# Partial logits and two ranking products moved to GpSimd, the gate's broadcast to ScalarE, fewer instructions for the gate's denominator

## The chip, the cores and the metric

The kernel runs on one core of a Trainium2 chip. A core has five engines that run their own instruction streams in program order and meet through semaphores: TensorE (PE; its weight loads are listed as PEld), VectorE (DVE), ScalarE (ACT), GpSimd (POOL) and SyncE (SP), whose queue issues most transfers. The metric is the device time of one execution in microseconds (us).

## The reference

Two stages with the arrays in fp32. The first is an attention through 32 memory slots for 8 batches and 8 heads of 576 positions; the second is a mixture of 8 experts in which every one of the 4608 tokens goes to the one expert with the largest logit.

```python
# attention, per batch and head
a = softmax(phi)                       # over the 576 positions
k_m, v_m = a.T @ k, a.T @ v            # 32 x 64 each
x = softmax(q @ k_m.T / 8) @ v_m       # over the 32 slots
# experts, on x as 4608 x 512
logits = x @ w_gate
e_idx = argmax(logits, axis=1)
probs = exp(logits - logits.max()); probs /= probs.sum() + 1e-9
gate_w = probs[e_idx]
eom = 1 / (1 + exp(-(x @ w_output_gate)))
out[t] = gate_w[t] * eom[t, e] * (relu(x[t] @ w1[e]) @ w2[e])
```

The factor of a token's row is therefore 1 / ((sum of exp(logit - max) + 1e-9) * (1 + exp(-z))), with z the chosen expert's output-gate logit.

## The kernel before

**Attention.** Batches are handled in four pairs (index `bp`), each in five steps of 256 or 128 positions, so 20 steps (`t` counts them, three more drain the pipeline). For one step `scores` makes the scores on PE; `shift` (lines 866 to 872) turns them by a VectorE transpose, takes a maximum on VectorE (L870) and subtracts it on GpSimd (L872); `expo` (L876) takes the exponential on ScalarE; `divide` (L882 to L885) sums and inverts on VectorE and multiplies on GpSimd (L885); `back` (L890) transposes back; `values` (L903, L905) multiplies by the value memories on PE and copies the result, `xo`, to SBUF on ScalarE; `store` (L1014, L1018) writes it to the scratch `xs` in DRAM. A row of `xs` has four quarters of 144 columns: 128 of x and 16 partial logits (8 of the gate, 8 of the output gate). `memory` meanwhile makes the next pair's memories (`kvm`, L782, on ScalarE; `ve_b`, L784, on GpSimd; two memsets, L727 and L728).

**Logits.** The 16 logits of a token are the sum of its four partial ones. `store` defers that sum (L1022, VectorE) by eight items of the list `ORDER`; it is then emitted right behind the next step's `shift`, and, for the last step of a pair, at once at the end of the step.

**Ranking.** After the last step of a pair, `rank(bp)` works out each token's expert (`oh`, one-hot), its place among that expert's tokens (`pr` on PE, L956 to L960), and its factor `gd`, which is copied to 16 columns (`gt`, L981) and written by four DMAs over the columns 128 to 143 of the first quarter in `xs` (L983, L986), where the experts' stage reads only column 128. It also makes nine 128 x 128 matrices `Aw` on GpSimd (L988). It is a generator: every `yield` gives the turn back to the rest of the program. For the second pair it is driven eight turns at the head of the next attention step, ahead of that step's `shift`; for the third it is driven by `hook`, two turns behind three items of attention. With the second and third pair runs `route_early`, which from `Aw` and the counts makes the lists of tokens (`table`, L233 to L250) by which the first blocks' rows are gathered (L538, GpSimd).

**Experts.** A block is up to 384 tokens of one expert; its rows are gathered from `xs`, transposed on PE (L1089), split into a high and a low part, and multiplied by weights that are split in the same way (`whl`: ScalarE L577, VectorE L591). L1241 is the first layer's matmul, L1278 the second's. The first block starts inside the attention's last part, so that the rest of the attention and of the ranking is emitted between the experts' matmuls. Since every engine works in program order, an instruction that waits holds all that stand behind it on its engine.

```python
ORDER = ["R4", "W", "X", "S", "R0", "m", "D", "M", "B", "V0", "R1", "R1", "V1", "M", "m", "C"]
LATE = {"lg": 8, "w": 2, "ct": 8, "pe": 3, "dve": 2}
```

In `ORDER`, R is turns of the ranking, X `expo`, S `shift`, D `divide`, B `back`, V `values` and `store`, C the next `scores`, m and M the memories.

Of the kernel before, what the change touches and what calls it, by code (L numbers as in the profile page):

```python
# [8 lines left out]
F32 = mybir.dt.float32  # L9
# [3 lines left out]
AF = mybir.ActivationFunctionType  # L13
ALU = mybir.AluOpType
AX = mybir.AxisListType
PSUM = bass.MemoryType.PSUM

P = 128
B, H, S, D, M = 8, 8, 576, 64, 32
NTOK, DM, E, F = 4608, 512, 8, 1024  # L20
NBP = B // 2
NCH = 9
# [37 lines left out]
XQ = 144  # L60
# [7 lines left out]
def attention_moe(tc, phiT, kv, qT, wgo, wall, out):  # L68
    nc = tc.nc
    V, A, G, T = nc.vector, nc.scalar, nc.gpsimd, nc.tensor  # L70

    with contextlib.ExitStack() as ctx:
        cp = ctx.enter_context(tc.tile_pool(name="cp", bufs=1))
        dp = ctx.enter_context(tc.tile_pool(name="dp", bufs=1, space=bass.MemoryType.DRAM))
        xs = dp.tile([NTOK, XROW], F32, name="xs")
# [27 lines left out]
        rt = ctx.enter_context(tc.tile_pool(name="rt", bufs=1))  # L103
# [52 lines left out]
        wg = cp.tile([P, H, 16], F32, name="wg")  # L156
        nc.sync.dma_start(wg[64:128], wgo)

        ohg = rt.tile([P, NCHT, E], BF16, name="ohg", bufs=1)
        jg = rt.tile([P, NCHT], I32, name="jg", bufs=1)  # L160
        Aw = rt.tile([P, NCHT, P], BF16, name="Aw", bufs=1)
# [299 lines left out]
        def take_pr():  # L461

            while taken:
                yield
            taken.append(1)

        def hold(n):

            if "open" not in env:
                return  # L470
            end = clock[0] + n
            while clock[0] < end:
                yield
# [433 lines left out]
        def rank(bp, lg):  # L907

            t0 = bp * 2 * S
            lt = lg[:, :, 0:E]  # L910
            lo = lg[:, :, E:2 * E]
            b3 = [P, NCH, E]
            cs = slice(bp * NCH, (bp + 1) * NCH)
            lm = rt.tile([P, NCH], F32, name="lm")
            w1_ = rt.tile(b3, F32, name="w1_")
            w2_ = rt.tile(b3, F32, name="w2_")
            w3_ = rt.tile(b3, F32, name="w3_")
            pm = rt.tile([P, NCH], F32, name="pm")
            zs = rt.tile([P, NCH], F32, name="zs")
            gd = rt.tile([P, NCH], F32, name="gd")  # L920
            oc = rt.tile([P, E], F32, name="oc")
            rki = rt.tile([P, NCH], I32, name="rki")
            ri = rt.tile([P, NCH], I32, name="ri")
            row = rt.tile([P, NCH], F32, name="row")
            gt = rt.tile([P, NCH, XQ - P], F32, name="gt")
            oh = ohg[:, cs]
            dscb = desc[:].unsqueeze(1).to_broadcast(b3)
            lmb = lm[:].unsqueeze(2).to_broadcast(b3)
            V.tensor_reduce(lm[:], lt, axis=AX.X, op=ALU.max)
            yield  # L930
            V.tensor_tensor(w1_[:], lt, lmb, ALU.is_ge)
            G.tensor_tensor(w2_[:], lt, lmb, ALU.subtract)
            yield
            V.tensor_tensor(w1_[:], w1_[:], dscb, ALU.mult)
            yield
            V.tensor_reduce(pm[:], w1_[:], axis=AX.X, op=ALU.max)
            yield
            V.tensor_tensor(oh, dscb, pm[:].unsqueeze(2).to_broadcast(b3), ALU.is_equal)
            yield
            V.tensor_reduce(oc[:], oh.rearrange("p c e -> p e c"), axis=AX.X, op=ALU.add)  # L940
            V.tensor_tensor(w3_[:], oh, lo, ALU.mult)
            A.activation(w2_[:], w2_[:], AF.Exp)
            yield
            if bp:
                V.tensor_tensor(ohcs[bp][:], ohcs[bp - 1][:], oc[:], ALU.add)
            else:
                V.tensor_copy(ohcs[bp][:], oc[:])
            V.tensor_reduce(zs[:], w3_[:], axis=AX.X, op=ALU.add)
            yield

            def rest():
                yield from take_pr()
                yield from hold(LATE["pe"])

                pr = ps_r.tile([P, NCH, E], F32, name="pr")
                T.matmul(pr[:], strict[:], oh, start=True, stop=False)  # L956
                if bp:
                    T.matmul(pr[:], ones_b[:], ohcs[bp - 1][:].unsqueeze(1).to_broadcast(b3), start=False, stop=False)
                for c in range(1, NCH):
                    T.matmul(pr[:, c:], ones_b[:], oh[:, 0:NCH - c], start=False, stop=(c == NCH - 1))  # L960
                yield
                V.tensor_reduce(gd[:], w2_[:], axis=AX.X, op=ALU.add)
                A.activation(zs[:], zs[:], AF.Exp, scale=-1.0)
                yield
                yield from hold(LATE["dve"])
                V.tensor_tensor(w1_[:], oh, pr[:], ALU.mult)
                taken.clear()
                V.tensor_scalar(gd[:], gd[:], 1e-9, None, ALU.add)
                yield
                with nc.allow_low_precision("whole numbers"):  # L970
                    V.tensor_reduce(rki[:], w1_[:], axis=AX.X, op=ALU.add)
                V.tensor_scalar(zs[:], zs[:], 1.0, None, ALU.add)
                yield
                V.tensor_scalar(ri[:], rki[:], 127, None, ALU.bitwise_and)
                V.tensor_scalar(jg[:, cs], rki[:], 7, None, ALU.arith_shift_right)
                V.tensor_tensor(gd[:], gd[:], zs[:], ALU.mult)
                yield
                V.tensor_copy(row[:], ri[:])  # L978
                V.reciprocal(gd[:], gd[:])
                yield  # L980
                V.tensor_copy(gt[:], gd[:].unsqueeze(2).to_broadcast([P, NCH, XQ - P]))  # L981
                for b in range(2):
                    nc.sync.dma_start(  # L983
                        xs[t0 + b * S:t0 + b * S + 512, P:XQ].rearrange("(c p) d -> p c d", p=P),
                        gt[:, 4 * b:4 * b + 4])
                    nc.sync.dma_start(xs[t0 + b * S + 512:t0 + b * S + 576, P:XQ], gt[64 * b:64 * b + 64, 8])  # L986
                for c in range(NCH):
                    (G if AWP else V).tensor_scalar(  # L988
                        Aw[:, bp * NCH + c], iota_row[:], row[:, c:c + 1], None, ALU.is_equal)
                    if c % 3 == 2:  # L990
                        yield
                ranked.append(bp)

            yield from together(route_early(bp - 1) if bp in (1, 2) else route_late() if bp == NBP - 1 else (), rest())

        ranked = []

        def together(*gens):

            gens = [iter(g) for g in gens]  # L1000
            while gens:
                for g in list(gens):
                    try:
                        next(g)
                    except StopIteration:
                        gens.remove(g)
                yield

        def store(bp, c2, xo, lg):
            t0 = bp * 2 * S  # L1010
            b, n = c2 // 2, 2 if c2 < 4 else 1
            if c2 < 4:
                r = t0 + b * S + (c2 % 2) * 256
                nc.sync.dma_start(xs[r:r + 256].rearrange("(c p) d -> p c d", p=P),  # L1014
                                  xo[:].rearrange("p c r d -> p c (r d)"))
            else:
                for b_ in range(2):
                    nc.sync.dma_start(  # L1018
                        xs[t0 + b_ * S + 512:t0 + b_ * S + 576],
                        xo[64 * b_:64 * b_ + 64, 0].rearrange("p r d -> p (r d)"))  # L1020
            xl = xo[:].rearrange("p c r (g d) -> p c (r g) d", g=2)[:, 0:n, :, P:XQ]
            defer("lg", lambda: V.tensor_reduce(  # L1022
                lg[:, 2 * c2:2 * c2 + n], xl.rearrange("p c q l -> p c l q"), axis=AX.X, op=ALU.add))

        def last(g):
            r = None
# [70 lines left out]
        def defer(nm, f):  # L1097
            deferred.append([LATE[nm], f])
# [15 lines left out]
        def attention():  # L1114
# [8 lines left out]
            for t in range(NT + LAG["V"]):  # L1123
# [45 lines left out]
                if g >= 0 and g % 5 == 4:  # L1169
                    bp = g // 5  # L1170
                    undefer(99)
                    left.append(bp)
                    rou.finish()
                    if bp < NBP - 1:
                        rou = Side(rank(bp, lgs[bp]))
                    else:
                        late.gens.append(rank(bp, lgs[bp]))
# [216 lines left out]
        n = NPE + NPT + NPP  # L1394
# [52 lines left out]
```

## Time and profile before

| | |
|---|---|
| median of 3 runs | 553.92 us (553.5 to 554.93) |
| the profiled execution's own time | 553.22 us |
| its span, first to last instruction | 551.5 us |
| PE busy | 507.9 us, 92% of the span |
| DVE busy | 354.1 us, 64% |
| ACT busy | 288.0 us, 52% |
| POOL busy | 231.8 us, 42% |
| mean granted TensorE clock | 0.97 |

A share of busy time is a mean over stages, so the stages are read one by one: a line of digits has the span in 40 slices of 13.8 us, each digit the busy share in tenths. A row of the timeline has the start, the length, the engine, the line of the program, the operation, the tile written and those read, and in square brackets how long the engine stood idle before it and who released it.

### The profile page before, as it was taken

Reading aid. Unit: us, or ns where it says so; the run is one execution under the profiler, and the core shown is the slowest. Engines: PE = TensorE matmul, PEld = TensorE weight load, DVE = VectorE, ACT = ScalarE, POOL = GpSimd, SP = SyncE. Lnnn points to the kernel's source line nnn. Section 1 sums busy time; section 2 is a strip of 40 time slices with the busy share of each in tenths; the row PEclk is TensorE's granted clock in tenths of the full one; section 3 lists DMA queues with packets and bytes.
Section 4 is the critical chain, followed back from the end, with each engine's and each line's share of the span. In section 5 each row is a group of like instructions: output and inputs, shape, how many; then the busy total and the mean of one; then the engine's idle time right before and its main releaser. Section 6 shows DMA issues by size and latency. Waiting matters only on the chain. (4 is left out here: it accounts for less than half of the span.)

```text
span 551.5 us, 10575 instructions
## 1 busy us (share of the span) xinstructions
PE 507.9 (92%) x3859; PEld 439.1 (80%) x3859; DVE 354.1 (64%) x779; ACT 288.0 (52%) x536; POOL 231.8 (42%) x254
## 2 busy tenths in 40 slices
PE   3788767689999999999999999999999999999993
PEld 2555545469789889898898989898999899888982
DVE  4376687877866659997454564954786387629310
ACT  3467465545535455553444545854785386548310
POOL 2244374860444134510467472655447363821101
PEclk9969799979999999999999999999999999999997
DMA  8999999995567756973466574876686577743001
GB/s 306 419 391 386 408 356 372 302 413 170 152 185 219 248 162 226 315 201 117 149 183 204 173 239 129 247 217 217 176 259 188 189 236 245 220 151 98 30 21 43
DMA packets 41998, 123.54 MB, mean 224 GB/s; under 512 B 10256, under 2 KB 10320, under 8 KB 41552
## 3 DMA queue, kind: packets, MB, share of 16 engines
q1 hardware_dynamic: 35136, 102.71, 56.5%
q0 software_dynamic: 6800, 20.06, 10.2%
q8 instruction: 32, 0.52, 0.4%
q14 instruction: 30, 0.25, 0.2%
HBM read 102.40 MB, written 20.35 MB: 223 GB/s over the span
## 5 line engine op out<-in xcount | busy, mean ns | idle before, releaser
L1278 PE MATMUL bps<-whl,hh 128*128 128x512 f32 x640 | 192.4, 393 | 0.0
L1241 PE MATMUL bps<-xh,whl 128*128 128x384 f32 x640 | 165.8, 336 | 0.0
L591 DVE TENSOR_TENSOR whl<-w,whl 128x1024 fp32r<-128x1024 f32 x112 | 138.2, 1239 | 10.9 <-ACT whl L577 10.8
L1278 PEld LDWEIGHTS bps<-whl,hh 128*128 128x128 f32 x640 | 119.9, 188 | 24.3 <-issue 0.2
L577 ACT CAST whl<-w 128x1024 fp32r<-128x1024 f32 x112 | 116.5, 1045 | 21.2 <-PE bps L1278 16.5
L1241 PEld LDWEIGHTS bps<-xh,whl 128*128 128x128 f32 x640 | 115.8, 188 | 1.1 <-ACT hh L1245 0.4
L532 POOL DMA_INDIRECT xg<-xs,idx_ql x84 | 97.3, 1158 | 25.6 <-issue 23.5
L1241 PE MATMUL bps<-xl,whl 128*128 128x384 f32 x320 | 107.0, 334 | 0.0
L1278 PE MATMUL bps<-whl,hl 128*128 128x512 f32 x240 | 93.7, 390 | 0.0
L1246 DVE SCALAR_TENSOR_TENSOR hl<-bps,hh 128x384 fp32r<-128x384 f32 x80 | 44.0, 554 | 60.3 <-ACT hh L1245 60.3
L1245 ACT ACTIVATE hh<-bps 128x384 fp32r<-128x384 f32 x80 | 38.9, 492 | 76.2 <-PE bps L1241 76.1
L1214 POOL DMA_INDIRECT out<-y,idx_ol x23 | 25.2, 1095 | 110.6 <-ACT y L1213 54.3
L1241 PEld LDWEIGHTS bps<-xl,whl 128*128 128x128 f32 x320 | 60.1, 188 | 0.3
L1278 PEld LDWEIGHTS bps<-whl,hl 128*128 128x128 f32 x240 | 45.1, 188 | 8.5
L1236 PE MATMUL bps<-xh,whl 128*128 128x384 f32 x128 | 37.7, 338 | 0.0
L872 POOL TENSOR_TENSOR ea<-ea,mx 128x512 f32<-128x512 f32 (+1 forms) x20 | 19.2, 960 | 43.3 <-DVE mx L870 39.0
L1237 PE MATMUL bps<-xh,whl 128*128 128x256 f32 x128 | 35.7, 279 | 0.0
L1213 ACT ACTIVATE y<-bps,gx 128x512 f32<-128x512 f32 x19 | 13.1, 687 | 40.0 <-PE bps L1278 33.4
L905 ACT COPY xo<-bpd 128x576 f32<-128x576 f32 x36 | 22.2, 641 | 21.4 <-PE bpd L903 9.7
L903 PE MATMUL bpd<-ve_b,aT 64*128 64x144 f32 (+1 forms) x320 | 28.6, 331 | 3.4 <-DVE ea L866 3.2
L1214 POOL DMA_INDIRECT out<-y,idx_ob x9 | 10.1, 1119 | 49.8 <-ACT y L1213 37.8
L988 POOL TENSOR_SCALAR Aw<-iota_row,row 128x128 bf16<-128x128 bf16 x36 | 26.0, 738 | 8.9 <-DVE row L978 8.9
(267 smaller groups left out, 588.2 us busy)
## 6 DMA issues: line engine op xcount, KB each, us to landing
w<-wall SPq DMA_DIRECT2D x112, 512.0 KB, 4.4
kvt<-kv SPq DMA_DIRECT2D x32, 512.0 KB, 8.1
xs<-xo SPq DMA_DIRECT2D x16, 576.0 KB, 7.4
qt<-qT SPq DMA_DIRECT2D x16, 512.0 KB, 8.5
ph<-phiT SPq DMA_DIRECT2D x3, 1152.0 KB, 11.7
kv<-kv SPq DMA_DIRECT2D x4, 512.0 KB, 8.5
xg<-xs,idx_ql POOLq DMA_INDIRECT x84, 4.5
ph<-phiT SPq DMA_DIRECT2D x4, 288.0 KB, 3.2
```

The costliest lines, as they stand in the source:

```text
L532: G.indirect_dma_start(out=z["xg"][:, k, XQ * b:XQ * b + XQ], out_offset=None, in_=xs[0:z["rows"]].rearrange("t (a q) -> (t a) q", a=4), i ...
L577: A.copy(hl[:, 0], w[:])
L591: V.tensor_tensor(hl[:, 1], w[:], hl[:, 0].bitcast(F32), ALU.subtract)
L903: T.matmul(px[to:to + n, r, sl], z["aT"][h, o:o + n], ves[2 * bp + b][h, g], start=True, stop=True)
L988: (G if AWP else V).tensor_scalar(Aw[:, bp * NCH + c], iota_row[:], row[:, c:c + 1], None, ALU.is_equal)
L1214: G.indirect_dma_start(out=out, out_offset=bass.IndirectOffsetOnAxis(ap=z["idx"][1][0:n, z["q0"] + k:z["q0"] + k + 1], axis=0), in_=y[0:n] ...
L1236: T.matmul(pb, w[:, 0, o:o + P], x[0][:, cc], start=(cc == 0), stop=False)
L1237: T.matmul(pb[:, 0:256], w[:, 1, o:o + P], x[0][:, cc, 0:256], start=False, stop=(cc == 3))
L1241: T.matmul(pb, w[:, b, o:o + P], x[a][:, cc, 0:n_], start=(n == 0), stop=(n == 11))
L1245: A.activation(h_[:, j], pb, AF.Relu)
L1246: V.scalar_tensor_tensor(l_[:, j], pb, 0.0, h_[:, j].bitcast(F32), ALU.max, ALU.subtract)
L1278: T.matmul(py[k], a, w[:, b, DM * f:DM * f + DM], start=(u == 4 and f == 0 and n == 0), stop=(u == 7 and f == 1 and n == len(ps) - 1))
```

## The change

The sum of the partial logits becomes two additions on GpSimd. In `rank`, the product of the maximum's mask with `desc` and the product of `oh` with the output-gate logits go from VectorE to GpSimd. The exponentials `w2_` get a ninth column per token chunk, which holds 1e-9 from the start, so that the sum over nine has the denominator; `1 +` and the product for the factor become one instruction. The broadcast `gt` has 4 columns instead of 16 and is made on ScalarE; the four DMAs write 4 columns.

```diff
+        w2t = rt.tile([P, NCH, E + 1], F32, name="w2t", bufs=1)
+        V.memset(w2t[:, :, E:], 1e-9)
...
-            G.tensor_tensor(w2_[:], lt, lmb, ALU.subtract)
-            yield
-            V.tensor_tensor(w1_[:], w1_[:], dscb, ALU.mult)
+            G.tensor_tensor(w2_, lt, lmb, ALU.subtract)
+            yield
+            G.tensor_tensor(w1_[:], w1_[:], dscb, ALU.mult)
...
-            V.tensor_tensor(w3_[:], oh, lo, ALU.mult)
+            G.tensor_tensor(w3_[:], oh, lo, ALU.mult)
...
-                V.tensor_reduce(gd[:], w2_[:], axis=AX.X, op=ALU.add)
+                V.tensor_reduce(gd[:], w2s[:], axis=AX.X, op=ALU.add)
...
-                V.tensor_scalar(gd[:], gd[:], 1e-9, None, ALU.add)
...
-                V.tensor_scalar(zs[:], zs[:], 1.0, None, ALU.add)
...
-                V.tensor_tensor(gd[:], gd[:], zs[:], ALU.mult)
+                V.scalar_tensor_tensor(gd[:], zs[:], 1.0, gd[:], ALU.add, ALU.mult)
...
-                V.tensor_copy(gt[:], gd[:].unsqueeze(2).to_broadcast([P, NCH, XQ - P]))
+                A.copy(gt[:], gd[:].unsqueeze(2).to_broadcast([P, NCH, 4]))
...
-            defer("lg", lambda: V.tensor_reduce(
-                lg[:, 2 * c2:2 * c2 + n], xl.rearrange("p c q l -> p c l q"), axis=AX.X, op=ALU.add))
+            def logits():
+                half = rt.tile([P, 2, 2, XQ - P], F32, name="half", bufs=1)[:, 0:n]
+                G.tensor_tensor(half, xl[:, :, 0:2], xl[:, :, 2:4], ALU.add)
+                G.tensor_tensor(lg[:, 2 * c2:2 * c2 + n], half[:, :, 0], half[:, :, 1], ALU.add)
+
+            defer("lg", logits)
```

No `yield` is added or taken away.

## Rows read from the trace of the kernel before

**Rows 1.** The span in 40 slices, from the page: PE's busy tenths.

```profile
PE   3788767689999999999999999999999999999993
```

**Rows 2.** Busy time of the engines in four stretches. Columns: stretch and length, then for PE, PEld, DVE, ACT and POOL the busy us and (x) the number of instructions, then the granted clock, the DMA engines' mean busy share and the GB/s.

```profile
61.50:85.00 23.50, 18.47 (x324) 12.93 (x324) 18.01 (x52) 14.30 (x36) 14.14 (x20) 0.79 1.02 370
85.00:119.00 34.00, 24.71 (x444) 17.03 (x436) 31.37 (x93) 18.44 (x38) 22.38 (x28) 0.90 0.98 358
119.00:160.00 41.00, 40.16 (x299) 34.11 (x298) 32.63 (x84) 20.24 (x34) 16.41 (x20) 1.00 0.61 189
160.00:545.00 385.00, 382.59 (x2082) 347.25 (x2080) 239.28 (x461) 201.41 (x352) 157.02 (x140) 1.00 0.59 185
```

**Rows 3.** Timeline of VectorE around the start of the second pair's ranking.

```profile
86.67 0.36 DVE L1022 TENSOR_REDUCE lg<-xo 128x32 f32<-128x128 f32 x1
...
87.84 0.65 DVE L890 STREAM_TRANSPOSE aT<-ea 128x512 f32<-128x512 f32 x1
88.46 0.26 DVE L1022 TENSOR_REDUCE lg<-xo 128x16 f32<-128x64 f32 x1
88.75 0.23 DVE L929 TENSOR_REDUCE lm<-lg 128x9 f32<-128x72 f32 x1
89.02 0.80 DVE L931 TENSOR_TENSOR w__1397<-lg,lm 128x72 f32<-128x72 f32 x1
...
90.12 0.23 DVE L936 TENSOR_REDUCE pm<-w__1397 128x9 f32<-128x72 f32 x1
...
91.25 0.71 DVE L866 STREAM_TRANSPOSE ea<-bpd 128x512 f32<-128x512 f32 x1
...
94.07 0.23 DVE L190 TENSOR_TENSOR tge<-pr,thr_e 128x104 f32<-128x104 f32 x1
```

**Rows 4.** Timeline of GpSimd over the same stretch and on to the first gathers.

```profile
86.89 1.05 POOL L872 TENSOR_TENSOR ea<-ea,mx 128x512 f32<-128x512 f32 x1 [3.46 <-DVE mx L870]
88.00 0.31 POOL L727 MEMSET a<- 64x256 f32 x1
...
88.63 1.04 POOL L885 TENSOR_TENSOR ea<-ea,sa 128x512 f32<-128x512 f32 x1
89.64 0.34 POOL L932 TENSOR_TENSOR w__1398<-lg,lm 128x72 f32<-128x72 f32 x1
...
97.71 5.50 POOL L988 TENSOR_SCALAR Aw<-iota_row,row 128x128 bf16<-128x128 bf16 x9
...
103.75 1.04 POOL L885 TENSOR_TENSOR ea<-ea,sa 128x512 f32<-128x512 f32 x1
105.31 1.25 POOL L538 DMA_INDIRECT xg<-xs,idx_ga  x1 [0.52 <-DVE i L248]
...
109.20 1.05 POOL L872 TENSOR_TENSOR ea<-ea,mx 128x512 f32<-128x512 f32 x1
```

**Rows 5.** Timeline of PE: three places of the same stretch at which it waited.

```profile
91.20 0.17 PE L276 MATMUL pr<-ohc,ones_b 128*128 128x8 bf16 x1 [1.69 <-DVE ohc L945]
...
94.35 0.19 PE L956 MATMUL pr<-ohg,strict 128*128 128x72 bf16 x1 [0.78 <-DVE tge L190]
...
111.22 0.59 PE L791 MATMUL bpa<-ident,kvm 128*128 128x128 f32 x2 [2.58 <-ACT kvm L782]
```

**Rows 6.** Timeline of ScalarE in the second pair's ranking.

```profile
94.14 0.21 ACT L963 ACTIVATE zs<-zs 128x9 f32<-128x9 f32 x1
95.50 0.64 ACT L905 COPY xo<-bpd 128x576 f32<-128x576 f32 x1 [1.14 <-PE bpd L903]
96.27 0.62 ACT L782 ACTIVATE kvm<-pk,rs 128x128 f32<-128x128 f32 x2
```

**Rows 7.** Busy time in stretches, columns as in rows 2: a short idle time of PE, a longer one, and what followed the longer one.

```profile
89.50:91.20 1.70, 0.01 (x2) 0.03 (x1) 1.56 (x8) 0.78 (x2) 0.48 (x2) 1.00 1.03 415
...
108.70:111.20 2.50, 0.00 (x0) 0.00 (x0) 2.50 (x1) 1.61 (x4) 2.47 (x3) 1.00 1.00 386
111.20:118.90 7.70, 6.61 (x61) 4.42 (x62) 7.15 (x15) 4.36 (x10) 4.29 (x5) 0.56 1.03 416
```

**Rows 8.** Timelines of VectorE, GpSimd and PE in the third pair's ranking, which lies inside the experts' stage.

```profile
137.41 0.22 DVE L934 TENSOR_TENSOR w__2048<-w__2048,desc 128x72 f32<-128x72 f32 x1
137.67 0.23 DVE L936 TENSOR_REDUCE pm<-w__2048 128x9 f32<-128x72 f32 x1
...
139.75 0.79 DVE L938 TENSOR_TENSOR ohg<-desc,pm 128x72 bf16<-128x72 f32 x1
...
137.64 1.05 POOL L872 TENSOR_TENSOR ea<-ea,mx 128x512 f32<-128x512 f32 x1 [4.30 <-DVE w__2048 L934]
...
140.60 0.19 PE L956 MATMUL pr<-ohg,strict 128*128 128x72 bf16 x1 [0.25 <-DVE ohg L938]
```

**Rows 9.** Timelines of VectorE in the first pair's ranking, and of GpSimd behind the first pair's `Aw`.

```profile
61.53 0.26 DVE L1022 TENSOR_REDUCE lg<-xo 128x16 f32<-128x64 f32 x1 [4.25 <-ACT xo L905]
...
69.22 0.23 DVE L966 TENSOR_TENSOR w__950<-ohg,pr 128x72 f32<-128x72 bf16 x1 [0.67 <-PE pr L960]
...
79.25 1.04 POOL L872 TENSOR_TENSOR ea<-ea,mx 128x512 f32<-128x512 f32 x1
```

**Rows 10.** The group of the logit sums, from the groups by line: count, then busy us and mean ns of one, then the idle time before them and its releaser.

```profile
L1022 DVE TENSOR_REDUCE lg<-xo 128x32 f32<-128x128 f32 (+1 forms) x20 | 6.8, 341 | 4.3 <-ACT xo L905 4.3
```

**Rows 11.** Busy time in one stretch, columns as in rows 2: the two microseconds in which the first pair's factors are being written.

```profile
80.00:82.00 2.00, 0.74 (x4) 0.40 (x4) 1.07 (x4) 1.14 (x3) 2.00 (x4) 0.85 1.03 245
```

More of the change, by code (lines that the diff above doesn't have):

```diff
@@ L915, in rank @@
             w1_ = rt.tile(b3, F32, name="w1_")
-            w2_ = rt.tile(b3, F32, name="w2_")
+            w2s = w2t
+            w2_ = w2s[:, :, 0:E]
             w3_ = rt.tile(b3, F32, name="w3_")
@@ L924, in rank @@
             row = rt.tile([P, NCH], F32, name="row")
-            gt = rt.tile([P, NCH, XQ - P], F32, name="gt")
+            gt = rt.tile([P, NCH, 4], F32, name="gt")
             oh = ohg[:, cs]
@@ L940, in rank @@
             V.tensor_reduce(oc[:], oh.rearrange("p c e -> p e c"), axis=AX.X, op=ALU.add)
-            V.tensor_tensor(w3_[:], oh, lo, ALU.mult)
-            A.activation(w2_[:], w2_[:], AF.Exp)
+            G.tensor_tensor(w3_[:], oh, lo, ALU.mult)
+            A.activation(w2_, w2_, AF.Exp)
             yield
@@ L980, in rest @@
                 yield
-                V.tensor_copy(gt[:], gd[:].unsqueeze(2).to_broadcast([P, NCH, XQ - P]))
+                A.copy(gt[:], gd[:].unsqueeze(2).to_broadcast([P, NCH, 4]))
                 for b in range(2):
                     nc.sync.dma_start(
-                        xs[t0 + b * S:t0 + b * S + 512, P:XQ].rearrange("(c p) d -> p c d", p=P),
+                        xs[t0 + b * S:t0 + b * S + 512, P:P + 4].rearrange("(c p) d -> p c d", p=P),
                         gt[:, 4 * b:4 * b + 4])
-                    nc.sync.dma_start(xs[t0 + b * S + 512:t0 + b * S + 576, P:XQ], gt[64 * b:64 * b + 64, 8])
+                    nc.sync.dma_start(xs[t0 + b * S + 512:t0 + b * S + 576, P:P + 4], gt[64 * b:64 * b + 64, 8])
                 for c in range(NCH):
```

## The prediction

> **What bounds the kernel now.** I read the page's 40 slices first [rows 1]: PE's digit is 6 to 8 in the early slices and 9 nearly throughout the rest. Then the windows [rows 2]: from 160 to 545 us PE is busy 382.59 of 385 us, so there whatever VectorE or GpSimd saves or loses is worth nothing unless PE stands still for it. PE idles before 119 us: 9.3 us between 85 and 119 (34.00 less 24.71), where VectorE is busy 31.37 of 34. So the time is the moment at which the experts' matmuls start (119 us) plus nearly fixed PE work, plus any hole that the change puts into PE later. The DMA engines are full up to 119 us (share 0.98 and 1.02), but the waits of PE in the stretch are on VectorE and ScalarE [rows 5], so I read the three timelines instruction by instruction.
>
> The chain from 85 us on is this. VectorE runs without a gap from L1022 to L190 [rows 3]. PE waits for it twice, at 91.20 for the counts (1.69 us) and at 94.35 for L190, which frees the bank `pr` [rows 5]. Behind L956 on PE stands `values`, then ScalarE's `xo` (95.50) and `kvm` (96.27) [rows 6], then GpSimd's L784 and the nine `Aw` (97.71), then the lists and the gathers (105.31), then L872 (109.20) [rows 4], whose exponential holds the `kvm` for which PE waits 2.58 us at 111.22 [rows 5]. What delays L190 delays the first expert matmul one for one.
>
> **Prices.** On GpSimd a product of 72 columns takes 0.34 us, a 256-column memset 0.31 [rows 4]. The new additions have 64 and 32 columns; I take 0.30 each, 0.6 a pair (bounds 0.5, a little under the memset for both, and 0.7, two products). On VectorE the sum that goes cost 6.8 us in 20 [rows 10], some 0.27 us of pitch each. The product by `desc` costs VectorE 0.22 [rows 8] against 0.34 on GpSimd. The Trainium skill (GPSIMD Engine Reference, 4.1 Engine selection) puts two-input elementwise work about two times slower on GpSimd than on VectorE; these rows have one and a half times. By the rule the product would be 0.45 and the sum below 0.2 us higher.
>
> **Part by part.** (a) *Before 85 us: -0.3 us.* In the first pair's ranking the maximum waits for two additions instead of one sum (+0.4) and then for the product's detour (+0.2). But VectorE waited 0.67 us for PE at 69.22 [rows 9], and that hides both. Behind it three small instructions and a sum leave VectorE ahead of `Aw`, whose end releases L872 at 79.25 [rows 9], so that chain comes some 0.3 us earlier (bounds 0 and -0.6). The additions behind that L872 lengthen GpSimd's own row of work, but nothing waits for its end before 85 us.
>
> (b) *Second pair's ranking: +1.8 us.* On GpSimd the order will be: L872, ending 87.94; the pair of additions for 86.67's sum, 88.54; the two memsets (0.63 from 88.00 to 88.63), 89.17; L885, 1.01, 90.18; the pair for 88.46's sum, 90.78; and only then can L929 start on VectorE, at 90.85 instead of 88.75 [rows 3, 4]: +2.1. VectorE is through with L890 by 88.2 and stands idle, with the whole ranking and the next `shift` (91.25) queued behind. L931 then no longer runs beside L885, so its 0.80 falls to some 0.23, but the product by `desc` must wait for L932 on GpSimd (0.34 + 0.34): from L929 to L936 it takes 1.07 us instead of 1.37, -0.3. The other product costs nothing net: 0.14 us leave VectorE and a wait of that size for GpSimd comes in. Left is +1.8 at L866, and the same at L190. Bounds: 1.4 (0.5 a pair, no latency) and 2.2.
>
> (c) *Behind it: +0.3 us.* The copy to `gt` is put into ScalarE's stream between `xo` and `kvm` (nearest row, L963 with 9 columns, 0.21 [rows 6]): +0.2, bounds 0 and 0.3. A pair of additions lies ahead of L885 at 103.75 and so of the gathers; they waited 0.52 for the lists there [rows 4], so of 0.6 some 0.1 shows (bounds 0 and 0.2).
>
> (d) *The clock: +0.6 us.* PE's idle time before L276 grows from 1.69 to some 3.4 us. After the 1.70 us without PE work from 89.50 the clock stayed at 1.00, while behind the 2.50 us from 108.70 it was 0.56 on average for 7.7 us, that is mostly the lower level of 1.2 GHz [rows 7]. So I expect the matmuls between L276 and L956 to run partly at 1.2 GHz. From 91.20 on PE had 3.41 us of work in 4.2; twice that time would be hidden in part by L190, which is late by 1.8 itself. Bounds 0 and 1.9; I take 0.6, a third, because L190 hides the first part.
>
> (e) *Third pair's ranking: +1.4 us.* It is in the experts' stage, where PE has no slack: already now L956 waited for `oh` at 140.60 [rows 8]. `hook` emits `shift` and then the ranking, so on GpSimd the product by `desc` stands behind L872 (137.64 to 138.69) and ends at 139.03; L936 starts at 139.1 instead of 137.67, with L1246, L882 and L938 behind it on VectorE. `oh` is 1.4 us later, and PE has nothing else to do ahead of L956. Bounds 1.1 and 1.7. What waits on the weights' split behind it moves with PE and costs nothing more.
>
> (f) *Nothing.* The fourth pair's ranking: GpSimd is free there and PE is covered by matmuls. The additions behind 160 us: PE covers them; if that cover went they would be 0.6 us each. The ninth column, the memset at the start and the fused factor: four small instructions fewer in each ranking, behind L190. The DMAs have as many packets as before, only shorter. While the first pair's were under way the core moved 245 GB/s [rows 11] against 370 in its stretch [rows 2], so at most 2 x (1 - 245/370) = 0.7 us a ranking could come back, and as much be lost; PE waits for none of it, so 0.
>
> Sum: -0.3 + 1.8 + 0.3 + 0.6 + 1.4 = +3.8 on the profiled execution's 553.22: **557.0 us**. That execution lies 0.7 below the median of the runs (553.92), which can come on top; the range has room for it.
>
> **The rivals.** *VectorE's relief decides (faster).* It is the engine busy 92% between 85 and 119 us, and the change takes from it there four sums' pitches of 0.27, and in the ranking 0.22 + 0.14 for the products, 0.22 for the copy and 0.15 for two small ones: 1.8 us, with (a) 2.1, so 551.1 us. It decides if the additions' results are there before VectorE has done L890 at 88.2; for that the last pair would have to run ahead of L885 on GpSimd. Against it speaks the order of the code: `divide` comes before `store`.
>
> *Off the path (about the same).* The delay before 119 us is swallowed, because the start of the experts hangs on transfers with the queues full up to there; only (a) and (e) stay: 553.22 - 0.3 + 1.4 = 554.3. For it speaks the DMA share of 0.98; against it that none of PE's waits in rows 5 ends with a DMA.
>
> *Two engines in each other's way (still slower).* L931 took 0.80 us beside L885 [rows 3] and the like operation 0.22 alone [rows 8]. The Trainium skill (GPSIMD Engine Reference, 8. Key points) says that GpSimd shares its SBUF interfaces with VectorE and contends with VectorE instructions that have two SBUF inputs; the rows agree. The new additions lie beside such instructions between 85 and 119 us perhaps once or twice at 0.58 each, say 0.6, and with the clock at its upper bound (+1.3) that gives 557.0 + 1.9 = 558.9.
>
> **How the numbers follow.** Slower as worked out 0.57 (own range 555.2 to 558.4), the upper rival 0.08, about the same 0.20, faster 0.15. Less than 0.3%, 1.7 us, cannot be told from no change here. The first two are slower but for 0.01 at the lower edge: slower 0.64, same 0.21, faster 0.15. The range reaches from 552.9, which takes in the middle case and leaves out most of the faster one, to 559.5 for the upper rival and the 0.7 us of the median.
>
> **What would show it.** Right: L929 of the second pair starts two us or more after L890 ends, released by GpSimd; PE's wait before L276 is 3 us or more and the clock falls behind it; L936 of the third pair waits for GpSimd, and L956 waits over 1 us inside the experts' stage; the first L1241 comes near 121.5 us instead of 119. Wrong: the additions take under 0.2 us, PE's first L1241 comes before 119, or L956 finds its input ready.

## The result: slower by 0.59%, and the profile after

| | before | after |
|---|---|---|
| median of 5 runs | 553.92 us (553.35 to 554.93) | 556.87 us (555.89 to 557.71) |
| ratio, 95% interval | 1 | 1.0059 [1.0041, 1.0077] |
| profiled execution, own time | 553.22 us | 557.38 us |
| its span | 551.5 us | 555.1 us |
| busy DVE, POOL, PE | 354.1, 231.8, 507.9 us | 345.1, 250.3, 513.3 us |

The forecast was 557.0 us. VectorE was relieved of 9 us, and the kernel became 3 us longer. In code and trace of after, most lines have numbers 2 to 5 higher (L932 is L929 of before, L937 is L934, L868 is L866, L278 is L276, L959 is L956, L1246 is L1241; L1025 and L1026 are the two additions).

First the stretches that answer to [rows 2], with borders moved along with the work (columns as there):

```profile
61.50:85.00 23.50, 19.78 (x328) 13.15 (x327) 15.96 (x43) 14.30 (x37) 15.88 (x29) 0.78 1.03 388
85.00:121.00 36.00, 27.81 (x436) 19.43 (x437) 27.96 (x82) 18.42 (x40) 28.19 (x45) 0.81 0.96 337
121.00:162.00 41.00, 38.87 (x292) 33.01 (x292) 30.36 (x71) 19.81 (x34) 20.02 (x29) 1.00 0.58 180
162.00:548.00 386.00, 383.89 (x2087) 348.26 (x2085) 239.01 (x458) 202.28 (x354) 162.56 (x149) 1.00 0.59 185
```

From 162 us on PE is busy 383.89 of 386, as it was 382.59 of 385: nothing changed there. Before that, PE's 9.3 us without work in the second stretch became 8.2 in one that is 2 us longer, with the clock at 0.81 instead of 0.90; the third has 2.1 us without work instead of 0.8.

The second pair's ranking on VectorE, answering to [rows 3], and the row that opens this step. Columns of every timeline: start, length, engine, line, operation, tiles, idle time before it and who ended it.

```profile
85.07 0.72 DVE L868 STREAM_TRANSPOSE ea<-bpd 128x512 f32<-128x512 f32 x1 [0.18 <-PE bpd L858]
...
87.32 0.65 DVE L892 STREAM_TRANSPOSE aT<-ea 128x512 f32<-128x512 f32 x1
90.56 0.23 DVE L932 TENSOR_REDUCE lm<-lg 128x9 f32<-128x72 f32 x1 [2.59 <-POOL lg L1026]
...
91.55 0.23 DVE L939 TENSOR_REDUCE pm<-w__1416 128x9 f32<-128x72 f32 x1 [0.50 <-POOL w__1416 L937]
...
92.63 0.70 DVE L868 STREAM_TRANSPOSE ea<-bpd 128x512 f32<-128x512 f32 x1
...
95.44 0.23 DVE L192 TENSOR_TENSOR tge<-pr,thr_e 128x104 f32<-128x104 f32 x1
```

On VectorE nothing runs between 87.97 and 90.56: L932 waits 2.59 us for the last addition. GpSimd shows why; answering to [rows 4]:

```profile
86.62 1.05 POOL L874 TENSOR_TENSOR ea<-ea,mx 128x512 f32<-128x512 f32 x1
87.63 0.33 POOL L1025 TENSOR_TENSOR half<-xo 128x64 f32<-128x64 f32 x1
88.03 0.25 POOL L1026 TENSOR_TENSOR lg<-half 128x32 f32<-128x32 f32 x1
88.35 0.31 POOL L729 MEMSET a<- 64x256 f32 x1
88.71 0.30 POOL L730 MEMSET a<- 64x256 f32 x1
88.98 1.04 POOL L887 TENSOR_TENSOR ea<-ea,sa 128x512 f32<-128x512 f32 x1
89.98 0.24 POOL L1025 TENSOR_TENSOR half<-xo 128x32 f32<-128x32 f32 x1
90.31 0.22 POOL L1026 TENSOR_TENSOR lg<-half 128x16 f32<-128x16 f32 x1
```

Two pairs of additions, two memsets and the multiplication L887 stand without a gap between the subtraction at 86.62 and the result at 90.53. Nothing here waits for data: the row is only long. PE, answering to [rows 5] and, for the third pair, to [rows 8]:

```profile
92.62 0.17 PE L278 MATMUL pr<-ohc,ones_b 128*128 128x8 bf16 x1 [3.33 <-DVE ohc L948]
...
95.75 0.24 PE L959 MATMUL pr<-ohg,strict 128*128 128x72 bf16 x1
...
113.32 0.59 PE L793 MATMUL bpa<-ident,kvm 128*128 128x128 f32 x2 [1.37 <-ACT kvm L784]
...
120.56 0.69 PE L1246 MATMUL bps<-xh,whl 128*128 128x384 f32 x1
...
143.75 0.19 PE L959 MATMUL pr<-ohg,strict 128*128 128x72 bf16 x1 [1.54 <-DVE ohg L941]
```

PE waits 3.33 us for the counts instead of 1.69, 1.37 instead of 2.58 for `kvm`, and inside the experts' stage 1.54 instead of 0.25 for `oh`. The first expert matmul is at 120.56, before at 118.98; the forecast put it near 121.5.

Absolute times of two profiles can't simply be subtracted: the second pair's step opens (VectorE's transpose L866 or L868 ahead of the ranking) at 84.48 to 87.49 us in the 14 profiles of this study, in no order that follows the kernels. Lengths between two events of one profile repeat better: of the four below A, C and D do within 0.3 us where two profiles have the same instructions in the same places, and B doesn't. The table has, for each kernel, from its timelines: A, from the start of that transpose to the start of the matmul of the counts (L276 or L278); B, from there to the first expert matmul; the granted clock over the 7 us behind the counts; C, from the first expert matmul to the third pair's L956 or L959; D, from there to the end of the last matmul; and the measured ratio.

| kernel | A | B | clock | C | D | ratio to before, 95% |
|---|---|---|---|---|---|---|
| before | 5.89 | 27.78 | 1.00 | 21.62 | 401.99 | |
| after | 7.55 | 27.94 | 0.76 | 23.19 | 402.14 | 1.0059 [1.0041, 1.0077] |
| after_again | 7.51 | 28.93 | 0.61 | 22.89 | 402.16 | 1.0060 [1.0037, 1.0083] |
| both_vector | 5.88 | 28.35 | 1.00 | 21.63 | 402.14 | 1.0009 [0.9994, 1.0024] |
| desc_vector | 7.34 | 28.53 | 0.60 | 21.62 | 402.14 | 1.0044 [1.0025, 1.0062] |
| sums_vector | 6.06 | 28.34 | 0.76 | 22.98 | 402.15 | 1.0051 [1.0029, 1.0072] |
| last_sum_vector | 6.41 | 28.25 | 1.00 | 22.10 | 402.14 | 1.0002 [0.9987, 1.0017] |
| desc_early | 7.50 | 27.63 | 0.76 | 21.34 | 402.16 | 1.0044 [1.0023, 1.0066] |
| order_only | 6.60 | 28.19 | 1.00 | 21.35 | 402.14 | 0.9999 [0.9975, 1.0023] |
| filler | 7.51 | 27.30 | 1.00 | 22.92 | 402.16 | 1.0037 [1.0018, 1.0056] |
| filler_again | 7.50 | 27.79 | 0.76 | 22.89 | 402.16 | 1.0041 [1.0024, 1.0059] |
| subtract_vector | 6.41 | 27.47 | 0.76 | 21.62 | 402.14 | 1.0026 [1.0000, 1.0051] |
| add_desc | 6.08 | 29.21 | 0.76 | 22.95 | 401.99 | 1.0018 [0.9998, 1.0037] |
| add_sums | 7.33 | 27.49 | 0.76 | 21.61 | 401.97 | 1.0021 [1.0004, 1.0037] |

The loss of after is in A (+1.6 to +1.7) and in C (+1.3 to +1.6), and 0.15 in D; B scatters over 1.9 us. A + C + D give +3.1 to +3.4 us (after_again and after); the ratio is worth +3.3 us of 553.92 (2.3 to 4.3). For each other kernel the same sum lies within its interval too (filler's at its upper end), but for last_sum_vector, where it gives 1.0021.

### The profile page after: what moved, and what is told of

It is laid out like the page before. It is cut to its first block, busy times and chain, and to the rows that moved or that the text cites. A ratio compares the mean times of both kernels' runs of the same rounds, so it can differ in the third digit from the quotient of the medians.

```text
span 555.1 us, 10579 instructions
## 1 busy us (share of the span) xinstructions
PE 513.3 (92%) x3859; PEld 441.9 (80%) x3859; DVE 345.1 (62%) x740; ACT 288.5 (52%) x540; POOL 250.3 (45%) x302
## 5 line engine op out<-in xcount | busy, mean ns | idle before, releaser
L1246 PE MATMUL bps<-xh,whl 128*128 128x384 f32 x640 | 166.0, 336 | 0.0
L593 DVE TENSOR_TENSOR whl<-w,whl 128x1024 fp32r<-128x1024 f32 x112 | 137.6, 1234 | 10.7 <-ACT whl L579 10.7
L579 ACT CAST whl<-w 128x1024 fp32r<-128x1024 f32 x112 | 116.5, 1045 | 19.7 <-PE bps L1283 16.3
L1246 PEld LDWEIGHTS bps<-xh,whl 128*128 128x128 f32 x640 | 116.0, 188 | 1.2 <-ACT hh L1250 0.4
L534 POOL DMA_INDIRECT xg<-xs,idx_ql x84 | 99.5, 1185 | 25.6 <-issue 23.8
L1246 PE MATMUL bps<-xl,whl 128*128 128x384 f32 x320 | 107.1, 335 | 0.0
L1246 PEld LDWEIGHTS bps<-xl,whl 128*128 128x128 f32 x320 | 60.2, 188 | 0.3
L1241 PE MATMUL bps<-xh,whl 128*128 128x384 f32 x128 | 37.7, 338 | 0.0
L874 POOL TENSOR_TENSOR ea<-ea,mx 128x512 f32<-128x512 f32 (+1 forms) x20 | 19.3, 964 | 40.0 <-DVE mx L872 34.2
L905 PE MATMUL bpd<-ve_b,aT 64*128 64x144 f32 (+1 forms) x320 | 30.0, 341 | 2.7 <-DVE ea L868 2.6
L868 DVE STREAM_TRANSPOSE ea<-bpd 128x512 f32<-128x512 f32 (+1 forms) x20 | 13.2, 659 | 29.1 <-PE bpd L858 29.1
```

Source lines behind the costliest of these rows:

```text
L534: G.indirect_dma_start(out=z["xg"][:, k, XQ * b:XQ * b + XQ], out_offset=None, in_=xs[0:z["rows"]].rearrange("t (a q) -> (t a) q", a=4), i ...
L579: A.copy(hl[:, 0], w[:])
L593: V.tensor_tensor(hl[:, 1], w[:], hl[:, 0].bitcast(F32), ALU.subtract)
L905: T.matmul(px[to:to + n, r, sl], z["aT"][h, o:o + n], ves[2 * bp + b][h, g], start=True, stop=True)
L1241: T.matmul(pb, w[:, 0, o:o + P], x[0][:, cc], start=(cc == 0), stop=False)
L1246: T.matmul(pb, w[:, b, o:o + P], x[a][:, cc, 0:n_], start=(n == 0), stop=(n == 11))
```

## The experiments

The theory: a moved instruction costs what its place in GpSimd's row costs, that is, what stands ahead of it there and who waits behind it; two places count, the last sum before the second pair's ranking (A) and the product by `desc` in the third pair's (C). Against it stand: the transfers and small edits (`gt` with 4 columns on ScalarE, the denominator); two engines in each other's way through the other 16 sums; the clock.

### One part or both put back on VectorE

```diff
# desc_vector, both_vector, last_sum_vector
-            G.tensor_tensor(w1_[:], w1_[:], dscb, ALU.mult)
+            V.tensor_tensor(w1_[:], w1_[:], dscb, ALU.mult)
# sums_vector, both_vector
-            defer("lg", logits)
+            defer("lg", lambda: V.tensor_reduce(
+                lg[:, 2 * c2:2 * c2 + n], xl.rearrange("p c q l -> p c l q"), axis=AX.X, op=ALU.add))
# last_sum_vector: the same only for the last step of a pair
+            defer("lg", logits if c2 < 4 else lambda: V.tensor_reduce(
...
```

**desc_vector.** 

> The changed kernel with the product by desc back on VectorE, everything else as changed. Order theory (the loss comes from where the moved instructions stand in GpSimd's program order): the hole of 1.54 us before L959 in the third pair's ranking closes to about 0.2, and in the second pair's ranking the wait of 0.50 for the product becomes 0.27 of VectorE's own work; 556.87 - 1.3 - 0.2 = 555.4 us. Interference theory (the loss comes from more two-input work on GpSimd beside VectorE's): 4 of 48 added GpSimd instructions leave, 556.6. Transfer theory (the shorter factor rows or the copy on ScalarE cost the time): 556.9.

Measured 556.28 us, 1.0044. C is back at 21.62, and A keeps 1.45 of its 1.66 us. The time is 0.9 us above the 555.4 expected: by the table 1.6 us should be left, 1.0029, where the interval begins at 1.0025. **sums_vector.** 

> The changed kernel with the sum of the partial logits back on VectorE, everything else as changed. Order theory: VectorE no longer stands 2.59 us before L932 of the second pair, PE's wait before L278 falls from 3.33 to about 1.9 us, the clock stays at 1.00 behind it, the experts start near 119.2 instead of 120.6 to 120.8 us; the hole before L959 stays at 1.5. 556.87 - 1.5 = 555.4, down to 554.9 if the clock was worth 0.5. Interference theory: 40 of 48 added instructions leave, 554.4. Transfer theory: 556.9.

Measured 556.03 us, 1.0051: less came back than either theory had, although A is down to 6.06 and only C stays (22.98). By the table 1.7 us should be left, 1.0031, at the lower end of the interval.

**both_vector.** 

> The changed kernel with the product by desc and the sum of the partial logits both back on VectorE; the product of the output gate's logits stays on GpSimd, the copy on ScalarE with 4 columns, the denominator in fewer instructions. Order theory: both holes gone, 553.5 to 554.0, that is the time of before or a little under it. Interference theory: 554.1. Transfer theory: 556.9, the loss stays.

Measured 553.37 us, 1.0009: the loss is gone, with `gt` on ScalarE, its 4 columns and the shorter denominator still in. These, and the product with the output-gate logits, are worth 0.15 us in the table (D); the interval leaves room for 1.3 us (1.0024), not for the loss of 3.3. The theory of the transfers falls. **last_sum_vector.** 

> The changed kernel with the product by desc on VectorE, and of the sums of partial logits only that of a pair's last step on VectorE; the other sixteen sums stay as two additions on GpSimd. Order theory: only the last sum is waited for at once, so this is as good as both sums and product on VectorE: 553.3 to 554.2. Interference theory: 36 of 48 added instructions stay, so about 556.1. Transfer theory: 556.9.

Measured 553.21 us, 1.0002. Sixteen of the twenty sums run on GpSimd, as in after, and cost nothing that these runs can measure (the table has +0.52 in A and, with the experts' first matmuls at a lower clock, +0.48 in C, which the ratio doesn't confirm); so the theory of engines in each other's way falls as a cause of the loss. They bring nothing either: VectorE's relief by these sixteen, some 4.3 us at 0.27 each, is in no term of the table.

### The same work on the same engines, in another order

```diff
# desc_early and order_only: the product is emitted one turn earlier
             G.tensor_tensor(w2_, lt, lmb, ALU.subtract)
-            yield
             G.tensor_tensor(w1_[:], w1_[:], dscb, ALU.mult)
             yield
+            yield
# order_only: divide's multiplication (L887) of the step ahead of a ranking
# is emitted behind the ranking's first turns
-            G.tensor_tensor(eav, eav, sa[:, 0:n].unsqueeze(2).to_broadcast([P, n, M]), ALU.mult)
+            def scale():
+                G.tensor_tensor(eav, eav, sa[:, 0:n].unsqueeze(2).to_broadcast([P, n, M]), ALU.mult)
+
+            if late_scale:
+                behind.append(scale)
+            else:
+                scale()
...
                             rou.step(int(w[1:]) * (2 if len(left) == 2 else 1))
+                        while behind and w == "R4":
+                            behind.pop(0)()
...
-                        divide(st[g])
+                        divide(st[g], t in (7, 12) and "open" not in env)
```

**desc_early.** 

> The changed kernel with one thing moved: the product by desc stays on GpSimd, but is emitted one turn earlier, right behind the subtraction, so that in the third pair's ranking it stands ahead of L874 in GpSimd's order instead of behind it. Same instructions on the same engines. Order theory: the hole before L959 closes from 1.54 to about 0.2 us although the product is still on GpSimd, and the time is that of the kernel with the product on VectorE, 1.004 times before. Interference theory, or a theory that a hop between engines is what costs: nothing changes, 1.006 times before.

Measured 555.2 us, 1.0044. GpSimd in the third pair's ranking, with the product (L936 here) ahead of the subtraction L874:

```profile
134.56 0.34 POOL L936 TENSOR_TENSOR w__2074<-w__2074,desc 128x72 f32<-128x72 f32 x1
139.13 1.05 POOL L874 TENSOR_TENSOR ea<-ea,mx 128x512 f32<-128x512 f32 x1 [4.23 <-DVE mx L872]
```

In after the product was at 140.45, behind an L874 that had come 1.01 us ahead of it; here it has run 4.57 us before L874, and C falls to 21.34, below that of before: `oh` is now early, and the small hole of 0.25 us that before had is gone too. A stays at 7.50.

**order_only.** 

> As before this one, and the multiplication of divide in the last step of the first and second pair (L887) is emitted behind the ranking's first turns, so that the last sum and the product stand ahead of it on GpSimd. All work stays on the changed kernel's engines. Order theory: VectorE's wait before L932 of the second pair falls from 2.59 to about 1.4 us (L874 and the memsets still stand ahead), PE's wait before its counts from 3.33 to about 2.2, the hole before L959 is closed: 1.002 to 1.003 times before. Interference theory: 1.006.

Measured 553.22 us, 0.9999 [0.9975, 1.0023]. GpSimd at the second pair's ranking:

```profile
88.86 0.25 POOL L1033 TENSOR_TENSOR half<-xo 128x32 f32<-128x32 f32 x1
89.19 0.22 POOL L1034 TENSOR_TENSOR lg<-half 128x16 f32<-128x16 f32 x1
89.76 0.36 POOL L943 TENSOR_TENSOR w2t<-lg,lm 128x72 f32<-128x72 f32 x1 [0.34 <-DVE lm L940]
90.08 0.33 POOL L944 TENSOR_TENSOR w__1415<-w__1415,desc 128x72 f32<-128x72 f32 x1
91.02 0.32 POOL L952 TENSOR_TENSOR w__1416<-ohg,lg 128x72 f32<-128x72 bf16 x1 [0.61 <-DVE ohg L949]
91.29 1.08 POOL L890 TENSOR_TENSOR ea<-ea,sa 128x512 f32<-128x512 f32 x1
```

The multiplication (L890 here) has gone from ahead of the last additions to 91.29, behind the ranking's instructions. L940 on VectorE, which is L932 of after, waits 1.65 us instead of 2.59:

```profile
89.45 0.23 DVE L940 TENSOR_REDUCE lm<-lg 128x9 f32<-128x72 f32 x1 [1.65 <-POOL lg L1034]
```

A is 6.60, 0.95 us less than after, and C 21.35. Every instruction stands on the engine where the change put it, with nearly the same length, and the loss of 3.3 us is gone, more of it than the 1.002 to 1.003 expected. This decides for the order. It doesn't beat the kernel before: A is still 0.71 above 5.89, C gains 0.27.

### One part alone, on the kernel before

The two parts by themselves: add_desc makes only the product by `desc` on GpSimd, add_sums only the sums. **add_desc.** 

> The kernel before with one edit: the product by desc on GpSimd. Order theory with two separate prices: a hole of about 1.5 us before L956 in the third pair's ranking (+1.3) and a wait of some 0.5 us in the second pair's (+0.2): 1.0027 times before. If the two moved parts only hurt together: 1.000 to 1.001.

Measured 554.63 us, 1.0018: A +0.19, C +1.33. **add_sums.** 

> The kernel before with one edit: the sums of the partial logits as two additions on GpSimd. Order theory with separate prices: VectorE waits some 2.6 us before L929 of the second pair, PE about 3.1 before its counts, the experts start 1.4 to 2 us later: 1.0025 to 1.0037 times before; the third pair's L956 keeps its wait of 0.25. If the two moved parts only hurt together: 1.000 to 1.001.

Measured 555.48 us, 1.0021: A +1.44, C unchanged. So the product's loss is mostly in the third pair's ranking and the sums' in the second's. **after_again** was the changed kernel once more beside these two. 

> The changed kernel itself once more, in the same session as the single parts, so that their ratios can be compared with its own: 1.0041 to 1.0077 times before, the interval of the first comparison. If the single parts above add up, it is the sum of their two losses.

Measured 557.8 us, 1.0060. The single losses add up to 0.0039; the difference to 0.0060 lies within the intervals, so whether the two cost more together stays open. The table's terms have no such surplus: in A 0.19 + 1.44 = 1.63 against 1.62 to 1.66, in C 1.33 against 1.27 to 1.57. The kernels made from after point the other way: over both_vector's 1.0009, the sums alone (desc_vector) cost 0.0035 and the product alone (sums_vector) 0.0042, together more than the 0.0050 of after. That the two losses add is thus read from the terms; the times are too scattered to show it.

### The clock

```diff
# filler, filler_again: PE works while it waits for the second pair's counts; what these write is overwritten
+            for _ in range(36 if bp == 1 else 0):
+                T.matmul(pr[:].rearrange("p c e -> p (c e)"), ones_b[:], strict[:, 0:NCH * E], start=True, stop=True)
             T.matmul(pr[:, 0], ones_b[:], ohcs[bp][:], start=True, stop=True)
```

**filler.** 

> The changed kernel with 36 extra matmuls of 72 columns on PE (about 1.6 us, their results overwritten) directly ahead of the second pair's counts, that is inside PE's wait of 3.33 us. If the lower clock behind that wait is a cost of its own (step d): the granted clock of the stretch behind the counts is 1.00 instead of 0.75, L959 comes right behind L192's release, the experts start 0.6 to 1.2 us earlier, about 555.9 us. If the clock costs nothing there because VectorE is late anyway: 556.9, no change; if the fillers themselves delay the counts: later.

Measured 555.8 us, 1.0037. **filler_again.** 

> The kernel with the 36 extra matmuls in PE's wait once more, beside the changed kernel in one session. If the lower clock behind the wait costs what the first comparison suggests, it stays 0.001 to 0.003 under the changed kernel's ratio; if that was scatter, the two are the same within 0.001.

Measured 556.04 us, 1.0041. The 36 matmuls took 1.34 us in both profiles. Behind the counts the clock stayed at 1.00 in the first and fell in the second; but in the first it had been at 0.50 from 83 to 89 us and had only just risen, so that the matmuls held it up isn't shown. The 7 us behind the counts, of filler and of after (columns as in [rows 2]), and filler's PE at the matmul that is L959 of after:

```profile
94.34:101.34 7.00, 5.91 (x124) 4.46 (x123) 6.83 (x34) 3.95 (x10) 3.32 (x4) 1.00 1.02 405
```

```profile
92.62:99.62 7.00, 7.00 (x122) 5.37 (x123) 6.69 (x35) 3.27 (x9) 2.65 (x4) 0.76 0.98 353
```

```profile
97.44 0.19 PE L961 MATMUL pr<-ohg,strict 128*128 128x72 bf16 x1 [0.74 <-DVE tge L192]
```

The matmuls of this stretch take PE 5.91 us at 1.00 and 7.00 at 0.76. Up to the ranking's matmul this costs nothing: filler's PE waits 0.74 us for L192 there and after's doesn't wait, yet from the counts it takes 3.10 us in one and 3.13 in the other. Nor does B follow the clock of these 7 us: it is 27.97 us on average in the five profiles with 1.00 and 27.98 in the seven with 0.76.

But the 7 us are a part of B, and in some profiles the clock falls a second time, or for longer, before the experts start. Over all of B its mean is 0.87 or 0.88 in seven profiles (before, both_vector, desc_early, order_only, filler, subtract_vector, add_sums), 0.82 in sums_vector and 0.71 to 0.77 in the other six. About the same matmuls keep PE busy for 20.6 to 21.1 us in the seven and 23.4 to 25.1 in the six, and B is 27.74 us on average in the seven and 28.44 in the six: 0.7 us more, with a 95% interval of 0.1 to 1.3, for groups made after the fact. The times point the same way. Of the 95 runs of the kernel before beside these experiments, the 36 with a mean clock over the execution of 0.966 or less took 554.14 us on average and the 35 with 0.972 or more 553.07, though a longer wait could itself lower the clock. Both filler ratios lie some 0.002 under after's, as expected; beside after_again the mean of the runs is 1.35 us shorter (95%: 0.2 to 2.5), yet in the profile of filler_again the clock did fall. So a price of the clock of the forecast's size, 0.6 us, is neither shown nor excluded.

### Another wait taken away

subtract_vector is last_sum_vector with one more edit: the subtraction L874 of step 16 runs on VectorE, since GpSimd does it behind the gathers, and PE's wait for `kvm` hangs on it in the kernel before [rows 4, 5].

```diff
-            G.tensor_tensor(eav, eav, mx[:, 0:n].unsqueeze(2).to_broadcast([P, n, M]), ALU.subtract)
+            eng.tensor_tensor(eav, eav, mx[:, 0:n].unsqueeze(2).to_broadcast([P, n, M]), ALU.subtract)
...
-                        shift(st[g])
+                        shift(st[g], V if g == 15 else G)
```

**subtract_vector.** 

> The kernel with the product and only the last sums on VectorE (1.000 times before), and in addition the subtraction of the sixteenth step's shift on VectorE, since on GpSimd it stands behind three gathers just before the experts start. Order theory carried further: ScalarE's exponential and with it kvm come up to 0.9 us earlier, PE's wait before the transposes of kvm falls from 2.6 us to under 2, the experts start up to 1.5 us earlier if the clock stays up behind it: 0.997 to 0.9995 times before. Rival: the experts' start is set by the gathered rows landing, then 1.000.

Measured 554.04 us, 1.0026: a miss. The rows of VectorE and ScalarE ahead of `kvm`, and of PE behind it:

```profile
108.17 0.69 DVE L874 TENSOR_TENSOR ea<-ea,mx 128x512 f32<-128x512 f32 x1
...
110.66 1.04 ACT L579 CAST whl<-w 128x1024 fp32r<-128x1024 f32 x1 [0.71 <-DMA w<-wall]
111.61 0.62 ACT L878 ACTIVATE ea<-ea 128x512 f32<-128x512 f32 x1
...
112.54 0.73 PE L793 MATMUL bpa<-ident,kvm 128*128 128x128 f32 x2 [2.40 <-ACT kvm L784]
...
117.53 0.98 PE L1095 MATMUL bps<-ident,xg 128*128 128x128 f32 x7 [0.84 <-DMA xg<-xs,idx_ga]
```

The subtraction ended at 108.86, but its exponential L878 stands behind the weights' conversion L579 on ScalarE, and that waited 0.71 us for the weights' transfer. So L878 comes at 111.61, 2.75 us behind the subtraction; in before it had waited for the subtraction itself. PE still waits 2.40 us for `kvm`, and then 0.84 us, where before had none, for the gathered rows. B is 27.47, within the range of the other profiles.

## Why the prediction was right, step by step

*(a) Before 85 us, -0.3.* The step opens 0.24 us earlier in after (85.07 against 85.31), but this start lies anywhere between 84.48 and 87.49 in 14 profiles. Not shown either way; the named chain, over the first pair's `Aw`, isn't seen to move: the subtraction behind `Aw` starts at 79.26 us in after and at 79.25 in before.

*(b) Second pair's ranking, +1.8.* Right, with each instruction where it was put. From the opening of the step L932 comes 2.05 us later (90.56 - 85.07 = 5.49 against 3.44; forecast 2.1), L932 to L939 takes 0.99 instead of 1.37, and the next step's L868 comes 1.62 later (7.56 against 5.94), A 1.66. The term that was a little too large is the last pair of additions: with 32 and 16 columns it took 0.24 + 0.22, not 0.6; the full pair took 0.32 + 0.25.

*(c) Behind it, +0.3.* Both parts were sized wrongly, and that their sum comes out near is luck. The copy `gt` didn't come between `xo` and `kvm`:

```profile
98.32 0.63 ACT L784 ACTIVATE kvm<-pk,rs 128x128 f32<-128x128 f32 x2
...
99.39 0.22 ACT L982 COPY gt<-gd 128x36 f32<-128x36 f32 x1
```

It stands behind `kvm` and costs nothing, where 0.2 was put. The gathers start 2.37 us behind the end of `Aw` instead of 2.10: +0.27, where 0.1 was put (after's GpSimd row, answering to the end of [rows 4]):

```profile
99.62 5.40 POOL L989 TENSOR_SCALAR Aw<-iota_row,row 128x128 bf16<-128x128 bf16 x9
...
105.55 0.32 POOL L1025 TENSOR_TENSOR half<-xo 128x64 f32<-128x64 f32 x1
105.95 0.26 POOL L1026 TENSOR_TENSOR lg<-half 128x32 f32<-128x32 f32 x1
106.17 1.04 POOL L887 TENSOR_TENSOR ea<-ea,sa 128x512 f32<-128x512 f32 x1
107.39 1.25 POOL L540 DMA_INDIRECT xg<-xs,idx_ga  x1 [0.17 <-issue]
```

L1025 and L1026 stand ahead of L887 with hardly a gap up to the first gather. In B, which scatters over 1.9 us, none of this can be told.

*(d) The clock, +0.6.* The wait was 3.33 us (forecast 3 or more) and the clock fell, as said. That L190 hides the first part was right too: from the counts to L959 it is 3.13 us (95.75 - 92.62), before 3.15, since the slower matmuls fill the 0.78 us for which PE waited for L190 in before. Whether what was slower behind it cost 0.6 us is open: B's difference of 0.7 us between the profiles with more and with less time at the lower clock, and the runs' times, fit it, but don't prove it.

*(e) Third pair's ranking, +1.4.* Right. VectorE and GpSimd of after, answering to [rows 8]:

```profile
139.44 1.05 POOL L874 TENSOR_TENSOR ea<-ea,mx 128x512 f32<-128x512 f32 x1 [4.53 <-DVE mx L872]
140.45 0.34 POOL L937 TENSOR_TENSOR w__2074<-w__2074,desc 128x72 f32<-128x72 f32 x1
...
140.82 0.23 DVE L939 TENSOR_REDUCE pm<-w__2074 128x9 f32<-128x72 f32 x1 [1.46 <-POOL w__2074 L937]
```

The product stands behind L874 and L939 waits 1.46 us for it. L959's wait grew from 0.25 to 1.54: +1.29. C grew by 1.57 in this profile, where the clock over C was 0.99, and by 1.27 in after_again, where it was 1.00 as in before.

*(f) Nothing.* Right but for 0.15 us in D, which every kernel made from after has and the two made from before have not. In after it builds up in steps of some 0.013 us within 130 us behind L959, without a wait of PE; what it comes from is open. The prediction counts four small instructions fewer in each ranking; by the diff two are gone and a third, the copy, is on ScalarE, which changes nothing in the sum.

The sum of what was shown is 1.66 + 1.3 to 1.6 + 0.15, some 3.1 to 3.4 us, against 3.8 forecast; (c) and (d) stood for 0.9 of it and can't be told from B's scatter, and (a)'s -0.3 isn't shown. That the forecast of 557.0 lies within 0.2 us of the median is luck: it adds 3.8 to a profiled execution that was 0.7 below the median of before, where the medians differ by 2.95, and the two differences offset each other. The mechanism of (b) and (e), 3.2 of the 3.8, is what was right. Of the rivals, the relief of VectorE failed where it was said to: the results of the additions would have had to be there at 88.2 and came at 90.53. Its own sum took four sums from VectorE between 85 and 119 us, where the trace has six; with six it would have said 550.6 us. Off the path: A's delay does reach the first expert matmul. This comes 35.49 us behind the step's opening in after and 33.67 in before; A + B is 35.41 on average in the seven kernels with an A of 7.3 or more and 34.42 in the other seven, 1.0 of the 1.3 us by which A differs. The upper rival saw contention that exists, but off the path.

## What to carry to other kernels

On an engine that works in order, the price of a moved instruction is its place: list what the receiving engine does just ahead of it, and who waits for the result. Here the last sums (0.46 us of work for the last pair) and a product of 0.34 cost 1.4 and 1.3 us, mostly for one multiplication and one subtraction of 1.05 us that stood ahead of them, and with the order changed nothing that could be measured. Relief of a busy engine is worth only what its own lateness costs at the next meeting point, and lengths within a profile show this, where absolute times of two profiles shift by up to 3 us.

## What the runs showed of the hardware that was not expected

Beside L593, a VectorE instruction with two SBUF inputs, the new GpSimd additions took four times as long. GpSimd's rows of after, VectorE's of the same stretch, and one of VectorE in before:

```profile
111.29 1.06 POOL L874 TENSOR_TENSOR ea<-ea,mx 128x512 f32<-128x512 f32 x1
112.29 1.31 POOL L1025 TENSOR_TENSOR half<-xo 128x64 f32<-128x64 f32 x1
113.69 1.12 POOL L1026 TENSOR_TENSOR lg<-half 128x32 f32<-128x32 f32 x1
```

```profile
111.00 2.44 DVE L593 TENSOR_TENSOR whl<-w,whl 128x1024 fp32r<-128x1024 f32 x1 [1.17 <-ACT whl L579]
113.36 1.33 DVE L593 TENSOR_TENSOR whl<-w,whl 128x1024 fp32r<-128x1024 f32 x1
```

```profile
108.48 2.86 DVE L591 TENSOR_TENSOR whl<-w,whl 128x1024 fp32r<-128x1024 f32 x1 [0.32 <-ACT whl L577]
```

The additions took 1.31 and 1.12 us instead of 0.32 and 0.25. Four of the 40 additions in after start beside an L593, and these took 0.88 to 1.31 us; the other 36 took 0.22 to 0.34. The Trainium skill (GPSIMD Engine Reference, 1. Specifications) says that GpSimd's SBUF interfaces are shared with VectorE, with contention where VectorE's instruction has two SBUF inputs; the trace agrees. The rows read as if the two engines took turns: the additions end at 113.60 and 114.81, 0.16 and 0.12 us behind the end of an L593. The first L593 ends 1.09 us behind the end of L874 (113.44 against 112.35), nearly its whole usual length of 1.23 (the mean of all 112 is 1.234). So what it lost it lost to L874 and not to the additions: in before, without them, the same instruction took 2.86 us and ended 1.09 us behind L872 (111.34 against 110.25 [rows 4]). Taking turns is read from these rows; no run tests it. last_sum_vector has the same rows of the additions (1.31 and 1.12 at 111.17 and 112.56) and a ratio of 1.0002, so here it cost nothing that could be measured.

The second surprise is that a fallen clock can cost nothing for a while. Behind PE's wait for the counts it was at 1.00 in five profiles (waits of 1.69, 1.68, 1.85 and 1.75 us in before, both_vector, last_sum_vector and order_only, and 1.36 in filler) and lower in the nine others (waits of 1.87 to 3.33 us), yet up to the ranking's matmul the slower matmuls only fill a wait for VectorE. Over longer stretches the price stays open, as said under the clock. In add_desc it was at 0.50, the lower level of 1.2 GHz, from 92 to 94 us, and near the upper one again in the next two us:

```profile
92.00:94.00 2.00, 2.00 (x32) 1.56 (x26) 1.93 (x8) 0.20 (x1) 1.89 (x2) 0.50 1.02 385
94.00:96.00 2.00, 2.00 (x40) 1.52 (x38) 1.31 (x14) 1.17 (x3) 0.17 (x1) 0.97 1.02 412
```
